# Other landing times for a planner's loads, and four moved or cut steps, in an attention, mixture-of-experts and MLP kernel

## The chip, the cores and the metric

The kernel runs on one core of a Trainium2 chip, as one launch. A core has five engines that each take their own list of instructions in order: TensorE (PE, matmuls; PEld is its weight load), VectorE (DVE), ScalarE (ACT), GpSimd (POOL) and SyncE (SP), whose list here holds only the starts of DMA transfers. They meet through semaphores. PE writes to PSUM, which has eight banks of 128 x 512 float32. The metric is the time of one execution in microseconds (us); three runs of the kernel before gave 623.84, 624.47 and 625.8, so the median is 624.47.

## The reference, cut to what matters

```python
# 1. attention: 2 batches, 8 heads, 576 positions, head size 64
rel = pos[:, None] - pos[None, :]
mask_plain = (rel >= 0) & (rel < 32)                          # heads 0 to 3
mask_dil = (rel >= 0) & (rel < 128) & (rel % 4 == 0)          # heads 4 to 7
attn = softmax(where(mask, q @ k.T / 8, -1e9)) @ v
x = attn as (1152 tokens, 512)
# 2. four experts, all of them for every token
p = domain_probs / (domain_probs.sum(-1, keepdims=True) + 1e-09)
for e in range(4):                                            # w1[e] 512x1024, w2[e] 1024x512
    out += p[:, e:e + 1] * (np.maximum(x @ w1[e], 0.0) @ w2[e])
# 3. second MLP
h = out @ w_in                                                # 512x2048
result = (h - np.tanh(h)) @ w_out                             # 2048x512, so 1152x512 float32
```

## The kernel before, in words

All products are made from operands split in a high and a low part; three matmuls (high by high, high by low, low by high) stand for one. The 1152 tokens are in two sets, set 0 of 512 and set 1 of 640. Both MLPs are walked through in slices `n` of 512 hidden columns: n = 0 to 9 belong to the four experts (0 and 1 for set 0 alone, their counterparts 8 and 9 for set 1 alone), n = 10 to 13 to the second MLP (13 is `LAST`). For a slice and a set g there are *h steps* (x by w1, 6 matmuls each, 256 columns for set 0 and 320 for set 1, gathered over several steps in PSUM sums that stay open) and *y steps* (hidden by w2, one step for each 128 tokens: 12 matmuls of 128 x 512 into one bank, which `y_sum` then adds on DVE into the tile `acc`). From slice 2 on the h steps use sums of blocks of x and w1, as in Strassen's method; six of their sums are then open at once, in six of the eight banks. `merge` puts the y steps of the slice before between the h steps: its tuple says behind how many h steps each y step stands (`FIRST`, `LATE`, `THEN`, and a literal tuple, before the loop over `steps`).

The attention of set 0 comes first. Its heads and tokens are cut in pieces: plain and dilated heads, each in two halves. `score(half, i, c)` computes scores, with i = 0 for plain and 1 for dilated; `soft`, `turn` and `use` are softmax, transposes and the product with v. Steps called with `P.fill` true, or through `fill`, may be laid in gaps: the h steps of slice 0 are the first dense work and serve as fill there. `warm` steps are matmuls on zeros that may stand in gaps (on ring `bank`). In the same stretch the weights of slices 0 and 1 arrive in `raw` tiles (512 KB each, ring of 4) and are split: the high part by a copy on ACT or DVE, the low part `w - high` by a subtraction on POOL or DVE. `emit_probs` reduces the loaded tile `pr` to `psum_r`, which gives the experts' weights `pn`.

During the experts, `d_pair(i)` decodes the second MLP's weights, 32 times: a DMA brings a tile of ring `att`, four DVE operations and one on ACT make a 128 x 512 tile `w` in one of the two slots of ring `single`, and a DMA writes `w` back to memory (`in<-att` and `out<-att` in the profile). The next decode that uses a slot must wait until its write has landed. Later `w_load` reads the decoded weights into `raw` like any others.

No order of instructions is written by hand. Every call is recorded as an operation with an estimated duration; then `Order` lays all operations: `deadlines` works out a due time for each from the PE list backwards (with `flight` as the time of a load), `lay` plays the program through a model (a load's data come at a landing time after one path of 395 KB per us, `DMA_US` behind its last byte) and takes for each engine the operation that can start first, by due time among equals, and `seek` tries shifted due times on the operations up to the end of slice 0 and keeps what the model finds no worse. `emit` then writes the instructions in the laid order. So a constant of the model moves instructions on all engines: it is no time on the chip, but it sets each engine's list. The list of PE follows the code except for fill and warm steps.

Of the kernel before, what the change touches and what calls it, by code (L numbers as in the profile page):

```python
# [219 lines left out]
class Program:  # L220


    TAIL = {"tensor": 0.24, "vector": 0.07, "scalar": 0.08, "gpsimd": 0.08, "sync": 0.0}
    DMA_US, DMA_RATE, DMA_AHEAD, DMA_DEEP = 1.35, 395.0e3, 0.45, 8

    DMA_SLOW, DMA_SLOW_RATE = 7.0, 250.0e3

# [161 lines left out]
class Order:  # L389
# [6 lines left out]
    def __init__(self, program, rounds=3):  # L396
        self.ops = program.ops
        self.program = program
        for o in self.ops:
            for b in o.before:  # L400
                self.ops[b].after.append(o.n)
        self.rings = []
        for o in self.ops:
            for t in o.tiles:
                if t.ring not in self.rings:
                    self.rings.append(t.ring)
        for ring in self.rings:
            ring.tiles.sort(key=lambda t: t.touch[0])
        self.follow = None
        self.all = program.ops  # L410
        self.from_, self.until = program.seek, program.until
        for _ in range(rounds):
            self.deadlines()
            self.lay()
        if program.seek:
            self.seek(program.seek, 1200)
        self.lay()

    def seek(self, limit, times):
# [61 lines left out]
        self.ideal = due  # L481

    def flight(self, o):
        return Program.DMA_US + o.data / Program.DMA_RATE if o.data else 0.0

    def lay(self, limit=None):

# [21 lines left out]
        while done < len(ops):  # L509
# [73 lines left out]
            if o.data:  # L583
                slow = max(path, o.end) < Program.DMA_SLOW
                path = max(path, o.end) + o.data / (Program.DMA_SLOW_RATE if slow else Program.DMA_RATE)
                come = path + Program.DMA_US
            o.landing = come
            if o.data:
                lands.append(come)
# [15 lines left out]
            for n in o.after:  # L605
                if n >= len(ops):
                    continue
                a = ops[n]
# [68 lines left out]
def tile_local_attention_moe_tanhshrink(  # L677
# [56 lines left out]
    def bank(loose=False):  # L734
        return Tile(bank_r, [128, 512], F32, loose=loose).view()
# [17 lines left out]
    def add(engine, out, a, b):  # L753
        engine.tensor_tensor(out=out, in0=a, in1=b, op=ALU.add)
# [825 lines left out]
    def y_step(kind, n, g, i):  # L1580
# [1 line left out]
        c = SETS[g][1] // 128 - 1 - i  # L1582
        first = 3 if n < EARLY else 2
        fs = {"y": range(NF), "ya": range(first), "yb": range(first, NF)}[kind]
        y = opened.pop((g, c)) if kind == "yb" else bank(P.fill)
        if kind == "ya":
            opened[g, c] = y
        for f in fs:
            hh, hl = (hts[g, f][:, i, c * 128:(c + 1) * 128] for i in range(2))
            whi, wlo = (w2t[n, f][:, i] for i in range(2))  # L1590
# [6 lines left out]
        if kind != "ya":  # L1597
            y_sum(n, g, c, y)

    def y_sum(n, g, c, y):  # L1600
        e = slices[seq[n][0]][2]
        ch = SETS[g][0] // 128 + c
        where = acc if e is not None else oacc
# [20 lines left out]
        elif new:  # L1624
            copy(t, y)
        else:
            k_ = 2 if n == LAST and g == 1 and c == 0 else 1
            for i in range(k_):
                cs = slice(i * DM // k_, (i + 1) * DM // k_)
                add(dve, t[:, cs], y[:, cs], t[:, cs])  # L1630
                if n == LAST:
                    dma(out[ch * 128:(ch + 1) * 128, cs], t[:, cs], 128 * 2048.0 / k_)

    def x2_step(g, kk):

# [39 lines left out]
            return h + [a0, a1, b0, b1] + cs[2:]  # L1675
        return h[:-1] + [a0] + h[-1:] + [a1] + cs[:1:-1] + [b0, b1]

    FIRST, LATE, THEN = (1, 2, 3, 4, 5), (3, 4, 5, 6, 8), (5, 7, 11, 13)
    steps = direct([("h", 0, 0, NF + i) for i in range(NF)], 0, 0)[:-2]
    for n in range(1, EARLY):  # L1680
        steps += direct(hs(n, 0), n, 0)
# [5 lines left out]
        steps += direct(hs(n, 1), n, 1)  # L1687
    steps += hs(N2 - 1, 1) + direct(merge(hs(N2, 0), ys(N2 - 1, 1), LATE), N2, 0) + hs(N2, 1)
    for n in range(N2 + 1, LAST + 1):
        first = (2, 3, 4, 5, 6) if n > N2 + 1 else LATE  # L1690
        steps += merge(hs(n, 0), ys(n - 1, 1), first) + merge(hs(n, 1), ys(n, 0), THEN)
    steps += ys(LAST, 1)

# [60 lines left out]
    def first_attention():  # L1754
# [13 lines left out]
        def use(half, i, c):  # L1768
            both[i].values(half, c)
# [24 lines left out]
        soft(2, 3)  # L1794
        P.fill = True
        score(1, 0)
        score(1, 1)
        P.fill = False
        turn(0)
        turn(1)  # L1800
# [5 lines left out]
        turn(3)  # L1806
        use(0, 1, 0)
        use(0, 1, 1)
        fill(*[("h", 0, 0, f) for f in range(NF)])
        soft(6)  # L1810
        turn(4)
# [159 lines left out]
```

## Time and profile before

| | value |
|---|---|
| runs | 623.84, 624.47, 625.8 us |
| profiled execution | 625.1 us, of it span 623.3 us |
| PE busy | 614.4 us, 99% of the span |
| PEld busy | 541.2 us, 87% |
| DVE, POOL, ACT busy | 62%, 51%, 49% |
| DMA over the span | 109 GB/s; 303, 366 and 311 GB/s in the first three fortieths |
| PE clock granted | full in all 40 slices |

In the timeline a line gives the start, the length, the engine, line 338 (where all engine operations are emitted; 743 for DMAs), the operation with `out<-in` tile names, shape and count, and in brackets the idle time before it with what ended it. Matmuls overlap at their ends, so the length of a PE group is longer than its share; what a step cost is the time from its start to the start of the next. A group whose count is below 12 or 6 has lost records, not matmuls.

### The profile page before, as it was taken

Reading aid. Unit: us, or ns where it says so; the run is one execution under the profiler, and the core shown is the slowest. Engines: PE = TensorE matmul, PEld = TensorE weight load, DVE = VectorE, ACT = ScalarE, POOL = GpSimd, SP = SyncE. Lnnn points to the kernel's source line nnn. Section 1 sums busy time; section 2 is a strip of 40 time slices with the busy share of each in tenths; the row PEclk is TensorE's granted clock in tenths of the full one; section 3 lists DMA queues with packets and bytes.
Section 4 is the critical chain, followed back from the end, with each engine's and each line's share of the span. In section 5 each row is a group of like instructions: output and inputs, shape, how many; then the busy total and the mean of one; then the engine's idle time right before and its main releaser. Section 6 shows DMA issues by size and latency. Waiting matters only on the chain.

```text
span 623.3 us, 10631 instructions
## 1 busy us (share of the span) xinstructions
PE 614.4 (99%) x4019; PEld 541.2 (87%) x4019; DVE 385.8 (62%) x726; ACT 305.0 (49%) x743; POOL 315.7 (51%) x281
## 2 busy tenths in 40 slices
PE   9999999999999999999999999999999999999997
PEld 5787798989888889889889889898898988998986
DVE  5855567976677877835425465446787677753652
ACT  7776774654334334414314355343774653551540
POOL 4767982854334425425425459763664662560220
PEclk9999999999999999999999999999999999999999
DMA  8993144254444555212102002330305224200012
GB/s 303 366 311 103 35 129 127 83 161 146 135 136 170 186 159 196 70 51 68 35 34 68 35 34 77 125 120 21 117 34 155 100 89 131 102 2 1 17 52 84
DMA packets 37554, 68.03 MB, mean 109 GB/s; under 512 B 4224, under 2 KB 12032, under 8 KB 37504
## 3 DMA queue, kind: packets, MB, share of 16 engines
q1 hardware_dynamic: 37216, 67.07, 32.9%
q8 instruction: 31, 0.51, 0.3%
q10 hardware_dynamic: 288, 0.30, 0.1%
q14 instruction: 19, 0.16, 0.1%
HBM read 56.61 MB, written 10.75 MB: 108 GB/s over the span
## 4 chain that ended last, share of the span: by engine, by line
PE 86%; DMA 7%; DVE 3%; issue 1%; POOL 1%; ACT 1%; SPq 1%; DVEq 0%; POOLq 0%; ACTq 0%
PE bank L338 86%; DMA raw<-in_moe_w_dram 3%; DMA out<-att 2%; DVE att L338 2%; DMA pr<-in_moe_domain_probs_dram 1%; DMA x<-in_k_dram 1%; DVE acc L338 1%; DMA in<-att 1%; SPq L743 1%; ACT w L338 0%; POOL w L338 0%; DVE w L338 0%; POOL att L338 0%; POOL x L338 0%; DVE bank L338 0%
## 5 line engine op out<-in xcount | busy, mean ns | idle before, releaser
L338 PE MATMUL bank<-w,h 128*128 128x512 f32 (+1 forms) x1392 | 324.6, 385 | 2.9 <-DVE acc L338 1.0
L338 PE MATMUL bank<-x,w 128*128 128x256 f32 (+2 forms) x1992 | 287.3, 298 | 0.9 <-DVE bank L338 0.9
L338 PEld LDWEIGHTS bank<-w,h 128*128 128x128 f32 (+1 forms) x1392 | 240.4, 184 | 54.9 <-DVE acc L338 2.1
L338 PEld LDWEIGHTS bank<-x,w 128*128 128x128 f32 x1992 | 277.7, 188 | 11.3 <-DVE bank L338 1.1
L338 POOL TENSOR_TENSOR w<-raw,w 128x512 fp32r<-128x512 f32 x102 | 135.9, 1344 | 146.0 <-ACT w L338 141.9
L338 ACT ACTIVATE h<-bank 128x320 fp32r<-128x320 f32 (+3 forms) x168 | 68.4, 421 | 78.8 <-PE bank L338 62.5
L338 DVE SCALAR_TENSOR_TENSOR acc<-bank,pn,acc 128x512 f32<-128x512 f32 x59 | 44.2, 749 | 67.8 <-PE bank L338 67.8
L338 DVE SCALAR_TENSOR_TENSOR att<-att 128x512 int32<-128x512 int32 (+1 forms) x96 | 84.1, 887 | 2.1 <-ACT att L338 0.5
L338 DVE TENSOR_TENSOR bank<-bank,p 128x320 f32<-128x320 f32 (+1 forms) x132 | 61.1, 466 | 33.3 <-PE bank L338 20.0
L338 ACT ACTIVATE w<-raw 128x512 fp32r<-128x512 f32 x108 | 66.9, 628 | 24.4 <-PE bank L338 22.6
L338 DVE SCALAR_TENSOR_TENSOR h<-bank,h 128x320 fp32r<-128x320 f32 (+2 forms) x124 | 55.6, 463 | 26.1 <-ACT h L338 24.8
L338 POOL TENSOR_TENSOR w<-sum,w 128x512 fp32r<-128x512 f32 x36 | 48.5, 1346 | 43.2 <-ACT w L338 42.1
L338 ACT ACTIVATE p<-bank 128x320 f32<-128x320 f32 (+1 forms) x88 | 35.6, 412 | 50.6 <-PE bank L338 49.7
L338 ACT ACTIVATE att<-bank 128x256 f32<-128x256 f32 (+3 forms) x78 | 32.6, 431 | 52.1 <-PE bank L338 42.3
L338 ACT ACTIVATE att<-att 128x512 f32<-128x512 f32 (+2 forms) x39 | 25.4, 655 | 37.5 <-DVE att L338 31.7
L338 DVE TENSOR_TENSOR acc<-bank,acc 128x512 f32<-128x512 f32 (+1 forms) x28 | 18.7, 670 | 30.9 <-PE bank L338 30.9
L338 POOL TENSOR_TENSOR sum<-raw 128x512 f32<-128x512 f32 x12 | 15.5, 1292 | 39.1 <-DMA raw<-in_moe_w_dram 19.0
L338 POOL TENSOR_TENSOR h<-att,h 128x256 fp32r<-128x256 f32 (+1 forms) x28 | 21.8, 801 | 25.4 <-ACT h L338 24.8
L338 ACT ACTIVATE w<-sum 128x512 fp32r<-128x512 f32 x36 | 22.6, 627 | 21.0 <-PE bank L338 16.5
L338 DVE TENSOR_SCALAR att<-att 128x512 int32<-128x512 int32 x32 | 16.4, 511 | 21.7 <-DMA out<-att 11.4
L338 POOL TENSOR_TENSOR att<-att,st 128x480 f32<-128x480 f32 (+1 forms) x20 | 18.9, 948 | 9.9 <-DVE st L338 9.4
L338 DVE TENSOR_TENSOR bank<-bank,att 128x256 f32<-128x256 f32 (+1 forms) x32 | 14.7, 463 | 10.1 <-ACT att L338 9.9
(73 smaller groups left out, 348.4 us busy)
## 6 DMA issues: line engine op xcount, KB each, us to landing
raw<-in_moe_w_dram SPq DMA_DIRECT2D x40, 512.0 KB, 3.9
att<-in_moe_w_in_dram SPq DMA_DIRECT2D x16, 512.0 KB, 4.4
att<-in_moe_w_out_dram SPq DMA_DIRECT2D x16, 512.0 KB, 4.5
in<-att SPq DMA_DIRECT2D x16, 256.0 KB, 4.1
out<-att SPq DMA_DIRECT2D x16, 256.0 KB, 4.1
raw<-in SPq DMA_DIRECT2D x8, 512.0 KB, 3.6
raw<-out SPq DMA_DIRECT2D x8, 512.0 KB, 3.7
h<-in_v_dram SPq DMA_DIRECT2D x7, 512.0 KB, 7.1
```

The lines of the kernel that those rows point to most:

```text
L338: getattr(self.engine, method)(**real)
L743: getattr(nc, queue).dma_start(out=a, in_=b)
```

## The change: landing times by stretch, a moved score, other merge places, a cut last chunk

`DMA_US` is no longer 1.35 us for every load but goes by the model's time: 1.35 until 12 us, 2.2 until 28, 3.2 until 42 and 2.8 after; `flight` has 2.5; `seek` makes 1000 tries instead of 1200. The second dilated score, `score(1, 1)`, is called behind the first values as fill. `LATE` and the literal tuple of `merge` change. The last y step of the program is made in two banks of 256 columns, each with its own add and write; `y_sum` gets the columns as an argument.

```diff
-    DMA_US, DMA_RATE, DMA_AHEAD, DMA_DEEP = 1.35, 395.0e3, 0.45, 8
+    DMA_RATE, DMA_AHEAD, DMA_DEEP = 395.0e3, 0.45, 8
+    DMA_US = (12.0, 1.35), (28.0, 2.2), (42.0, 3.2), (9e9, 2.8)
...
-            self.seek(program.seek, 1200)
+            self.seek(program.seek, 1000)
...
     def flight(self, o):
-        return Program.DMA_US + o.data / Program.DMA_RATE if o.data else 0.0
+        return 2.5 + o.data / Program.DMA_RATE if o.data else 0.0
...
-                come = path + Program.DMA_US
+                come = path + next(us for until, us in Program.DMA_US if path < until)
...
+        if (n, g, c) == (LAST, 1, 0):
+            for i in range(2):
+                y = bank()
+                for f in fs:
+                    hh, hl = (hts[g, f][:, j, c * 128:(c + 1) * 128] for j in range(2))
+                    whi, wlo = (w2t[n, f][:, j, i * 256:(i + 1) * 256] for j in range(2))
+                    with P.group():
+                        for m, (a, b_) in enumerate(((hh, whi), (hh, wlo), (hl, whi))):
+                            pe.matmul(
+                                out=y[:, :256], lhsT=a, rhs=b_,
+                                start=(f == 0 and m == 0), stop=(f == NF - 1 and m == 2),
+                            )
+                y_sum(n, g, c, y[:, :256], slice(i * 256, (i + 1) * 256))
+            return
...
-            k_ = 2 if n == LAST and g == 1 and c == 0 else 1
-            for i in range(k_):
-                cs = slice(i * DM // k_, (i + 1) * DM // k_)
-                add(dve, t[:, cs], y[:, cs], t[:, cs])
-                if n == LAST:
-                    dma(out[ch * 128:(ch + 1) * 128, cs], t[:, cs], 128 * 2048.0 / k_)
+            add(dve, t[:, cs], y, t[:, cs])
+            if n == LAST:
+                dma(
+                    out[ch * 128:(ch + 1) * 128, cs], t[:, cs], 512.0 * (cs.stop - cs.start),
+                )
...
-    FIRST, LATE, THEN = (1, 2, 3, 4, 5), (3, 4, 5, 6, 8), (5, 7, 11, 13)
+    FIRST, LATE, THEN = (1, 2, 3, 4, 5), (3, 4, 5, 7, 9), (5, 7, 11, 13)
...
-        first = (2, 3, 4, 5, 6) if n > N2 + 1 else LATE
+        first = FIRST if n > N2 + 1 else LATE
...
         score(1, 0)
-        score(1, 1)
         P.fill = False
...
         use(0, 1, 1)
+        P.fill = True
+        score(1, 1)
+        P.fill = False
         fill(*[("h", 0, 0, f) for f in range(NF)])
```

What the constants move shows in the engines' lists. On SP, the two v tiles of the first halves and both w1 tiles of slice 0 now stand ahead of the q tile (256 KB) and the two k tiles (192 KB each) of the second dilated half, with the first w2 tile between those k tiles; before, the q and k tiles came first. On PE, three warm matmuls are added (10 for 7). The PE list has 12 matmuls of 512 columns fewer and 24 of 256 more.

The DVE list near the 25th us, before; `w2` and `raw` are the weights of slice 0, `x0` a block of set 0's x that PE waits for:

```order
L338 TENSOR_REDUCE psum_r_530<-pr_421 128x9
L338 TENSOR_TENSOR w2_455<-raw_253,w2_455 128x512
L338 TENSOR_TENSOR w2_532<-raw_262,w2_532 128x512
L338 TENSOR_TENSOR psum_r_530<-psum_r_530,eps_81 128x9
L338 TENSOR_TENSOR x0_364<-bank_534,x0_359 128x256
```

and now:

```order
L340 TENSOR_TENSOR w2_437<-raw_236,w2_437 128x512
L340 TENSOR_REDUCE psum_r_543<-pr_424 128x9
L340 TENSOR_TENSOR w2_530<-raw_303,w2_530 128x512
L340 TENSOR_TENSOR x0_338<-bank_534,x0_327 128x256
L340 SCALAR_TENSOR_TENSOR h0_583<-bank_453,h0_583 128x256
L340 TENSOR_TENSOR psum_r_543<-psum_r_543,eps_75 128x9
```

One of the two subtractions that stood behind the reduction of `pr` stands ahead of it, and the addition of `eps` behind the block of x.

The DVE list near the 175th us, before; `att` are steps of two decodes, `acc1` the sums of set 1's y steps, whose banks they give back:

```order
L338 SCALAR_TENSOR_TENSOR acc1_1776<-bank_2255,pn_594,acc1_1776 128x512
L338 TENSOR_SCALAR att_1483<-att_2193 128x512
L338 TENSOR_SCALAR att_1483<-att_2272 128x512
L338 SCALAR_TENSOR_TENSOR acc1_1776<-bank_2291,pn_594,acc1_1776 128x512
L338 SCALAR_TENSOR_TENSOR att_1483<-att_2272,att_1483 128x512
L338 SCALAR_TENSOR_TENSOR att_1483<-att_2193,att_1483 128x512
```

and now:

```order
L340 SCALAR_TENSOR_TENSOR acc1_1770<-bank_2260,pn_614,acc1_1770 128x512
L340 SCALAR_TENSOR_TENSOR acc1_1770<-bank_2292,pn_614,acc1_1770 128x512
L340 TENSOR_SCALAR att_1489<-att_2188 128x512
L340 TENSOR_SCALAR att_1489<-att_2275 128x512
L340 SCALAR_TENSOR_TENSOR att_1489<-att_2275,att_1489 128x512
L340 SCALAR_TENSOR_TENSOR att_1489<-att_2188,att_1489 128x512
```

The first two operations of the next pair of decodes have gone behind one more sum.

The PE list in the last slice, before; 128x256 rows are h steps of set 0 into their sums, 128x512 rows y steps of set 1:

```order
L338 MATMUL bank_6184<-x0_4136,w1_5972 128x256 x6
L338 MATMUL bank_6192<-w2_5774,h1_5978 128x512 x3
L338 MATMUL bank_6192<-w2_5780,h1_6014 128x512 x3
L338 MATMUL bank_6192<-w2_5791,h1_6034 128x512 x3
L338 MATMUL bank_6192<-w2_5799,h1_6048 128x512 x3
L338 MATMUL bank_6207<-x0_4136,w1_5972 128x256 x6
L338 MATMUL bank_6216<-w2_5774,h1_5978 128x512 x3
L338 MATMUL bank_6216<-w2_5780,h1_6014 128x512 x3
L338 MATMUL bank_6216<-w2_5791,h1_6034 128x512 x3
L338 MATMUL bank_6216<-w2_5799,h1_6048 128x512 x3
L338 MATMUL bank_6100<-x0_4123,w1_6003 128x256 x6
```

and now:

```order
L340 MATMUL bank_6201<-x0_4139,w1_5979 128x256 x6
L340 MATMUL bank_6209<-w2_5764,h1_5984 128x512 x3
L340 MATMUL bank_6209<-w2_5770,h1_6017 128x512 x3
L340 MATMUL bank_6209<-w2_5776,h1_6037 128x512 x3
L340 MATMUL bank_6209<-w2_5786,h1_6051 128x512 x3
L340 MATMUL bank_6231<-x0_4139,w1_5979 128x256 x6
L340 MATMUL bank_6103<-x0_4126,w1_6006 128x256 x6
L340 MATMUL bank_6132<-x0_4126,w1_6006 128x256 x6
```

The last y step (6216, now 6209) has gone from behind the h step that opens the sixth sum (6207, now 6231) to ahead of it.

## Rows read from the trace of the kernel before

**Rows 1.** The page: an engine's busy time, share and instructions.

```profile
PE 614.4 (99%) x4019; PEld 541.2 (87%) x4019; DVE 385.8 (62%) x726; ACT 305.0 (49%) x743; POOL 315.7 (51%) x281
```

**Rows 2.** Timeline of PE, 0 to 60 us: start, length, operation, idle before.

```profile
11.65 0.89 PE L338 MATMUL bank<-x,x 64*64 64x96 f32 x32
...
17.04 0.39 PE L338 MATMUL bank<-w,h 96*64 96x64 f32 x6 [0.72 <-issue]
...
17.76 5.24 PE L338 MATMUL bank<-x,w 128*128 128x256 f32 x42
...
28.90 1.68 PE L338 MATMUL bank<-w,h 128*128 128x512 f32 x6 [0.83 <-DVE x L338]
...
54.20 0.64 PE L338 MATMUL bank<-ident,att 128*96 128x128 f32 x4 [0.35 <-POOL att L338]
```

**Rows 3.** Timeline of DVE, around the reduction of `pr`.

```profile
25.46 0.19 DVE L338 TENSOR_REDUCE psum_r<-pr 128x9 f32<-128x36 f32 x1 [0.27 <-DMA pr<-in_moe_domain_probs_dram]
...
25.57 2.86 DVE L338 TENSOR_TENSOR w<-raw,w 128x512 fp32r<-128x512 f32 x2
...
28.43 0.41 DVE L338 TENSOR_TENSOR x<-bank,x 128x256 fp32r<-128x256 f32 x1
```

**Rows 4.** Timeline of DVE, the second w1 tile's first use.

```profile
17.20 0.43 DVE L338 CAST w<-raw 128x512 fp32r<-128x512 f32 x1 [0.52 <-DMA raw<-in_moe_w_dram]
```

**Rows 5.** Windows: busy time by engine, clock, DMA share, GB/s.

```profile
10.00:20.00 10.00, 8.93 (x141) 7.33 (x137) 7.25 (x23) 8.55 (x30) 6.51 (x7) 1.00 1.03 392
```

**Rows 6.** DMA view, 0 to 30 us: KB each, median from issue to landing.

```profile
h<-in_v_dram SPq DMA_DIRECT2D x4, 512.0 KB, 9.0
```

**Rows 7.** Timeline of POOL, 30 to 60 us.

```profile
50.66 1.29 POOL L338 TENSOR_TENSOR sum<-raw 128x512 f32<-128x512 f32 x1 [4.26 <-DMA raw<-in_moe_w_dram]
```

**Rows 8.** Timeline of PE, 156 to 190 us.

```profile
176.45 0.88 PE L338 MATMUL bank<-x,w 128*128 128x256 f32 x6
177.16 2.95 PE L338 MATMUL bank<-w,h 128*128 128x512 f32 x12
179.96 0.87 PE L338 MATMUL bank<-x,w 128*128 128x256 f32 x6
181.15 3.05 PE L338 MATMUL bank<-w,h 128*128 128x512 f32 x12 [0.32 <-DVE acc L338]
184.22 3.09 PE L338 MATMUL bank<-x,w 128*128 128x256 f32 x24
188.23 2.04 PE L338 MATMUL bank<-x,w 128*128 128x256 f32 x15 [0.92 <-DVE bank L338]
```

**Rows 9.** Timeline of DVE, 156 to 190 us.

```profile
178.65 0.43 DVE L338 TENSOR_SCALAR att<-att 128x512 int32<-128x512 int32 x1 [3.59 <-issue]
180.01 0.43 DVE L338 TENSOR_SCALAR att<-att 128x512 int32<-128x512 int32 x1 [0.93 <-DMA in<-att]
180.35 0.74 DVE L338 SCALAR_TENSOR_TENSOR acc<-bank,pn,acc 128x512 f32<-128x512 f32 x1
```

**Rows 10.** Timeline of PE at four places of the second MLP's merges.

```profile
423.74 0.86 PE L338 MATMUL bank<-x,w 128*128 128x256 f32 x6
424.74 2.60 PE L338 MATMUL bank<-w,h 128*128 128x512 f32 x10
...
473.98 0.86 PE L338 MATMUL bank<-x,w 128*128 128x256 f32 x6
474.83 2.36 PE L338 MATMUL bank<-w,h 128*128 128x512 f32 x9
...
524.35 0.86 PE L338 MATMUL bank<-x,w 128*128 128x256 f32 x6
525.92 3.05 PE L338 MATMUL bank<-w,h 128*128 128x512 f32 x12 [0.71 <-DVE acc L338]
...
572.68 0.86 PE L338 MATMUL bank<-x,w 128*128 128x256 f32 x6
573.63 3.05 PE L338 MATMUL bank<-w,h 128*128 128x512 f32 x12
```

**Rows 11.** Timeline of DVE, the last two adds of the program.

```profile
619.85 0.76 DVE L338 TENSOR_TENSOR acc<-bank,acc 128x256 f32<-128x256 f32 x2 [2.09 <-PE bank L338]
```

More of the change, by code (lines that the diff above doesn't have):

```diff
@@ L1584, in y_step @@
         fs = {"y": range(NF), "ya": range(first), "yb": range(first, NF)}[kind]
-        y = opened.pop((g, c)) if kind == "yb" else bank(P.fill)
+        if (n, g, c) != (LAST, 1, 0):
+            y = opened.pop((g, c)) if kind == "yb" else bank(P.fill)
         if kind == "ya":
             opened[g, c] = y
+        if (n, g, c) == (LAST, 1, 0):
[12 more added lines that the diff above has]
+            return
         for f in fs:
@@ L1598, in y_step, with y_sum @@
             y_sum(n, g, c, y)
-    def y_sum(n, g, c, y):
+    def y_sum(n, g, c, y, cs=slice(0, DM)):
         e = slices[seq[n][0]][2]
```

## The prediction

> **What bounds the kernel now.** I read the page first: PE is busy for 614.4 of 623.3 us [rows 1], so what can be won lies in the rest, or in PE steps that run longer than their like. Busy time hides the second kind, because matmuls overlap: between 423.74 and 424.74 no idle time is given before the next group, yet the h step there took 1.00 us from start to start [rows 10], where the same step from 176.45 to 177.16 took 0.71 [rows 8]. So next I went through the PE timeline by starts and compared every step with its like: 0.71 us for an h step of 6 matmuls of 256 columns, and 2.80 for a y step of 12 of 512 (177.16 to 179.96) [rows 8]. Excess stands in three places: the head up to 60 us (waits of 0.72, 0.83 and 0.35) [rows 2], 180 to 188 us [rows 8], and four h steps of the second MLP [rows 10]. Last I read the engine that PE waits for at each of them, DVE or POOL [rows 3, 7, 9]. The clock is full throughout, 1.00 in the stretch shown [rows 5], so no term here is one of clock.
>
> The profiled execution took 625.1 us (span 623.3, and 1.8 around it), 0.6 over the median of 624.47. I take all differences from the trace and put them on the median.
>
> **The change part by part.**
>
> *Head.* At 28.90 PE has waited 0.83 us for a block of x [rows 2]. DVE made it at 28.43, behind the reduction of `pr` (25.46, after a wait for its load) and two subtractions of weights that took 2.86 together, 1.43 each [rows 3]. In the new DVE list one of the two stands ahead of the reduction, where DVE had been waiting, and the addition of `eps` stands behind the block. If `pr` lands as before, what follows it is 0.19 + 1.43 + 0.41, so the block is there at 27.5; with a subtraction of up to 1.77, when POOL works beside it, at 27.85. PE must come earlier too: it came at 28.07 (28.90 less 0.83). The dilated scores that moved, 0.89 us at 11.65, stand ahead of the first dense step no more, and the wait of 0.72 at 17.04, which I put on a v tile still under way, goes because that tile is loaded sooner; 17.76 becomes about 16.15 [rows 2]. The 0.89 comes back between the dense steps, so PE is some 0.75 ahead at 28 and waits at 27.3. It starts at 27.55 to 27.85 instead of 28.90: 1.05 to 1.35 won, taken as 1.2.
>
> Are the weights there at 16.15? The second w1 tile was first used at 17.20, as it landed [rows 4]. Now 640 KB less stand ahead of it, at 392 GB/s [rows 5] 1.67 us, so it lands near 15.5. The moved k tiles now have the same bytes ahead as that tile had before, without one k tile (192 KB, 0.5 us) for the first, and with a w2 tile (512 KB, 1.3 us) for the second: 16.7 and 18.5. PE wants them behind one h step (16.9) and behind three more and the first scores (19.1). Both are covered, by a few tenths only. Bounds: all that PE can win here is 28.90 less 27.3, 1.6; if a k tile is late by 1.3 us more than this the head ends 0.5 later than before.
>
> *POOL at 54.* PE waited 0.35 [rows 2] for a multiply on POOL queued behind a sum that had itself waited 4.26 for a load [rows 7]. In the new POOL list that multiply stands ahead of the sum: 0.35 won. Bound below: nothing, if the softmax ahead of it is late instead.
>
> *Decoding.* DVE stands still from 174.6 to 178.65 and again to 180.01, for a slot of `single` whose write is under way [rows 9]; the sum queued behind comes only at 180.35, and PE, whose y step needs that sum's bank, starts at 181.15 instead of 180.67. The h step at 179.96 thus took 1.19 (0.48 over its like), the y step 3.07 (0.27 over), and the four h steps from 184.22 took 4.01 against 2.84 (1.17 over), ending in a wait for DVE [rows 8]: 1.92. With one more sum ahead of the waiting operations, that sum no longer waits for a write, and the first two excesses, 0.75, go. The third is a backlog: the sum after that one was begun at 183.42 before; now it follows three steps of the decode from 180.44 on, at 0.62 each, so at 182.3, 1.1 earlier, which is nearly the 1.17. I take 0.95 of it, so 1.7. Queued behind the waiting operations now: one sum fewer and the same bank additions. Bounds 0.75 to 1.92.
>
> *Merges.* Six sums of the h steps hold six banks, so two are left for y steps. The y step behind the sixth opened sum needs the bank of the y step ahead, whose add on DVE (0.74 for a like one [rows 9]) is not done in one h step of 0.71. That is the excess of 0.29, 0.14, 0.86 and 0.24 at the four places [rows 10], 1.53, and the y step behind runs 3.05 instead of 2.95 at the two where all its records are there, +0.1 each. In the new order the last y step stands ahead of the sixth sum in three slices, and in the fourth two h steps lie between. All goes: 1.53 + 0.2 = 1.7, bounds 1.4 and 1.95 (0.1 at all four).
>
> *The last chunk.* The two adds that end the program take 0.76 together [rows 11]; of 256 columns each, one now runs beside the second bank's matmuls, and the rest is 0.42. That wins 0.34. The 12 matmuls of 512 took 2.80, and 24 of 256, at 0.71 for 6, take 2.84 [rows 8]: 0.04 lost. With up to 0.05 for the change of bank I take 0.25 won, bounds 0.1 and 0.34. The Trainium skill, "TensorE: Matmul & The Clock Gate", section "Back-to-back issue gap", speaks against this edit: it says that a sustained stream costs about 81 ns a matmul at 128 columns and about 131 ns at 512. Between the two, an estimate from that page is 98 ns for 256, so 24 of these would cost 0.77 us more than 12 of 512, and the edit would lose 0.4. The rows measure 118 and 233 ns, nearly in the ratio of the columns, since the three float32 passes are no such stream; the sum by the page would be 0.65 us higher than mine.
>
> *What may be late next.* The new lists have tight places too: weight splits between sums of set 1 late in the second MLP, a chain of three decodes near 125 us with little slack, and three more warm matmuls, which only pay where PE waits anyway. None shows in a row of before. I take 0.4 lost, with 0 and 1.5 as ends; the upper is near the largest stall that such a chain caused here, 1.17 [rows 8].
>
> Sum: -1.2 - 0.35 - 1.7 - 1.7 - 0.25 + 0.4 = -4.8, from 624.47 to **619.7 us** (in the profiled execution's own terms 620.3).
>
> **The rivals.**
>
> *A: the head wins more.* PE comes earlier at every place of the head, and the remaining waits go as well: 1.6 instead of 1.2, and 0.3 of further waits, with the other terms at their good ends (1.92, 1.95, 0.34, and no new stall). -1.6 - 0.3 - 0.35 - 1.92 - 1.95 - 0.34 = -6.5, so 618.0. For it: each term is read from a wait that is in the trace. Against it: the softmax between is a chain over ACT, DVE and POOL, DVE and ACT are the busiest engines of the second ten microseconds after PE [rows 5], and starting PE sooner does not shorten it.
>
> *B: the landing constants do nothing on the chip.* They change what the planner believes, not when data land. If `pr` and the v tiles land so that the head's gain is taken back at the next wait, and the writes of decoded weights stall DVE at another sum, only merges and last chunk remain: -1.7 - 0.25 + 0.4 = -1.55, so 622.9. For it: DVE's waits at 178.65 and 180.01 are for transfers [rows 9], which an order of DVE does not shorten. Against it: both moved places have PE work beside the wait now.
>
> *C: slower, by the moved k tiles.* PE takes its list in order, so a k tile that lands late stops the dense steps behind it as well. If the tile lands not by the bytes ahead of it but with the rest of what is queued then, as late as `pr` did (25.46 [rows 3]), PE waits from 19.1 to 25.5, 6.4 us, and the head's 1.2 is lost: -4.8 + 1.2 + 6.4 = +2.8, so 627.3. It turns the sign from a landing at 22.7 on. For it: v tiles of that stretch took 9.0 us from issue to landing [rows 6], and another such delay behind these would do. Against it: issued near 9.5, 9.0 more is 18.5, the same as by bytes. The Trainium skill, "DMA: Bandwidth & Descriptors", section "Queues, rings and completion order", says that completion is not first in, first out for an issuing engine, so a landing by bytes ahead is not assured; no row here separates the two.
>
> **How the numbers follow.** A change of under 0.3%, 1.9 us, can't be told from none. The forecast has a chance of 0.60, its own range 618.0 to 621.5; A has 0.12, B 0.20, C 0.08. Of B a third counts as faster (better than 622.6), the rest as same. So faster is 0.60 + 0.12 + 0.07 = 0.79, same 0.13, slower 0.08. The range goes from 617.2, below A by a little since its terms may add to more, to 623.3, which holds most of B and leaves out C.
>
> **What would show it.** Right: no wait of PE for x near 28, with `pr`'s reduction between the two subtractions; dense steps from about 16.2; no gap at 54; y steps of 2.80 and h steps of 0.71 right through 180 to 188 us; in the second MLP's merges all h steps of set 0 at 0.71; one add of 256 columns behind the last matmul. Wrong: PE waiting at the moved scores for a load (C), the head ending no sooner than before although it starts dense sooner (B), a new wait for DVE where decodes stand, or 24 matmuls at the end that take more than 2.95.

## The result, and the profile after

Six runs of the changed kernel took 618.73 to 619.66 us, median 619.18; six of the kernel before, beside them, had a median of 624.79. The ratio is 0.9907, with a 95% interval of 0.9891 to 0.9922: 0.8 to 1.1% faster, beyond the 0.3% set as the bound of noise. Against the 624.47 that the forecast started from, it is 5.3 us; against the runs beside it, 5.6. The forecast was 619.7, the profiled execution 619.3 (forecast in those terms: 620.3).

The page of the changed kernel: engine shares, then the shares of the chain of work that ended last. The last line is that chain in the kernel before.

```profile
PE 612.9 (99%) x4034; PEld 542.4 (88%) x4034; DVE 375.2 (61%) x726; ACT 307.8 (50%) x743; POOL 317.7 (51%) x281
...
PE 98%; DVE 1%; ACT 0%; POOL 0%; issue 0%; DVEq 0%; POOLq 0%; ACTq 0%
```

```profile
PE 86%; DMA 7%; DVE 3%; issue 1%; POOL 1%; ACT 1%; SPq 1%; DVEq 0%; POOLq 0%; ACTq 0%
```

PE's busy time fell by only 1.5 us [rows 1]; the rest of the 5.8 us of span was time between steps. The chains tell more: that of the kernel before held 7% of DMA and 86% of PE, this one holds no DMA.

The PE timeline after, at the places of [rows 2]:

```profile
16.42 1.00 PE L340 MATMUL bank<-x,w 128*128 128x256 f32 x6
17.36 0.56 PE L340 MATMUL bank<-x,x 64*64 64x96 f32 x16
17.85 1.68 PE L340 MATMUL bank<-x,w 128*128 128x256 f32 x12
19.46 0.56 PE L340 MATMUL bank<-x,x 64*64 64x96 f32 x16
19.95 3.11 PE L340 MATMUL bank<-x,w 128*128 128x256 f32 x24
...
28.24 1.65 PE L340 MATMUL bank<-w,h 128*128 128x512 f32 x6
...
53.00 0.60 PE L340 MATMUL bank<-ident,att 128*96 128x128 f32 x4
```

No row has a wait left. The dense steps start at 16.42 (before: 17.76), the step of 28.90 at 28.24, that of 54.20 at 53.00. Its DVE and POOL queues, against [rows 3, 7]:

```profile
25.74 0.19 DVE L340 TENSOR_REDUCE psum_r<-pr 128x9 f32<-128x36 f32 x1 [0.88 <-DMA pr<-in_moe_domain_probs_dram]
...
26.80 0.41 DVE L340 TENSOR_TENSOR x<-bank,x 128x256 fp32r<-128x256 f32 x1
```

```profile
46.42 1.29 POOL L340 TENSOR_TENSOR sum<-raw 128x512 f32<-128x512 f32 x1 [0.63 <-DMA h<-in_v_dram]
...
50.15 1.00 POOL L340 TENSOR_TENSOR att<-att,st 128x480 f32<-128x480 f32 x1
```

The block of x is ready at 27.2, a microsecond before PE comes. `pr` even landed later than before (25.74 for 25.46), and it no longer matters. On POOL the sum starts at 46.42 instead of 50.66, so PE's multiply is not held up behind it. (Its row names a v tile as what ended the wait; the sum's own tile was issued at 39.64, where before it was issued at 43.87, and took 6.7 us to land in both.)

The stretch of the decodes, PE and DVE, against [rows 8, 9]:

```profile
175.77 2.94 PE L340 MATMUL bank<-w,h 128*128 128x512 f32 x12
178.54 0.88 PE L340 MATMUL bank<-x,w 128*128 128x256 f32 x6
179.26 2.96 PE L340 MATMUL bank<-w,h 128*128 128x512 f32 x12
182.06 8.15 PE L340 MATMUL bank<-x,w 128*128 128x256 f32 x65
...
192.83 2.95 PE L340 MATMUL bank<-w,h 128*128 128x512 f32 x12
```

The last of these y steps, in the kernel before:

```profile
196.29 2.96 PE L338 MATMUL bank<-w,h 128*128 128x512 f32 x12
```

DVE in the changed kernel:

```profile
175.26 0.75 DVE L340 SCALAR_TENSOR_TENSOR acc<-bank,pn,acc 128x512 f32<-128x512 f32 x1 [2.73 <-PE bank L340]
176.78 0.43 DVE L340 TENSOR_SCALAR att<-att 128x512 int32<-128x512 int32 x1 [0.77 <-DMA in<-att]
177.46 0.43 DVE L340 TENSOR_SCALAR att<-att 128x512 int32<-128x512 int32 x1 [0.25 <-DMA in<-att]
```

DVE's waits for the writes are 0.77 and 0.25 where they were 3.59 and 0.93, and PE runs through. PE was 1.39 us ahead of before at the y step of 177.16 (now 175.77) and 3.46 ahead at that of 196.29 (now 192.83): this stretch took 17.06 us instead of 19.13, so it gave 2.07 against this one trace of before.

In the second MLP, against [rows 10, 11]: one of the merges, the one new wait, and the end.

```profile
520.38 2.94 PE L340 MATMUL bank<-w,h 128*128 128x512 f32 x12
523.15 7.15 PE L340 MATMUL bank<-x,w 128*128 128x256 f32 x58
...
457.26 3.30 PE L340 MATMUL bank<-x,w 128*128 128x320 f32 x24 [0.37 <-DVE bank L340]
...
613.14 0.42 DVE L340 TENSOR_TENSOR acc<-bank,acc 128x256 f32<-128x256 f32 x1 [0.72 <-PE bank L340]
614.55 0.42 DVE L340 TENSOR_TENSOR acc<-bank,acc 128x256 f32<-128x256 f32 x1 [0.99 <-PE bank L340]
```

### The profile page after: what moved, and what is told of

Same layout as the page of the kernel before. It is cut to its first block, busy times and chain, and to the rows that moved or that the text cites. A ratio compares the mean times of both kernels' runs of the same rounds, so it can differ in the third digit from the quotient of the medians.

```text
span 617.5 us, 10655 instructions
## 1 busy us (share of the span) xinstructions
PE 612.9 (99%) x4034; PEld 542.4 (88%) x4034; DVE 375.2 (61%) x726; ACT 307.8 (50%) x743; POOL 317.7 (51%) x281
## 4 chain that ended last, share of the span: by engine, by line
PE 98%; DVE 1%; ACT 0%; POOL 0%; issue 0%; DVEq 0%; POOLq 0%; ACTq 0%
PE bank L340 98%; DVE x L340 0%; ACT att L340 0%; DVE bank L340 0%; DVE st L340 0%; POOL att L340 0%; DVE acc L340 0%; DVE att L340 0%; DVE h L340 0%; DVE zero L340 0%; DVEq L340 0%; POOLq L340 0%; ACTq L340 0%
## 5 line engine op out<-in xcount | busy, mean ns | idle before, releaser
L340 PE MATMUL bank<-w,h 128*128 128x512 f32 (+2 forms) x1404 | 323.5, 383 | 0.0
L340 ACT ACTIVATE h<-bank 128x320 fp32r<-128x320 f32 (+4 forms) x168 | 69.0, 422 | 79.7 <-PE bank L340 65.7
L340 DVE SCALAR_TENSOR_TENSOR att<-att 128x512 int32<-128x512 int32 (+1 forms) x96 | 73.1, 777 | 1.3
L340 ACT ACTIVATE att<-att 128x512 f32<-128x512 f32 (+2 forms) x39 | 25.3, 658 | 22.7 <-DVE att L340 16.9
L340 ACT ACTIVATE acc<-bank 128x512 f32<-128x512 f32 (+4 forms) x27 | 12.9, 505 | 11.7 <-PE bank L340 11.2
```

The source lines that it names most:

```text
L340: getattr(self.engine, method)(**real)
```

## The experiments

Each ran beside the kernel before on its chip. The ratios of whole times have intervals of 0.2 to 0.7 percentage points in width, so terms under 1 us are read from traces. A trace shows a single wait to a few hundredths, but only of its own execution. The ratio is the one on record; it is not the quotient of the two medians and differs from it by up to 0.1 percentage points. Where two orders of a list are compared, the operations were moved after the planner had laid everything else, so nothing else moves; a move gives an operation, by its number, a start behind another's.

**s_head: DVE's order near 25 us alone.** (78 is the reduction of `pr`, 79 to 81 the rest of the probabilities.)

```diff
+        for n, behind in ((78, 360), (79, 328), (80, 79), (81, 80)):
+            self.ops[n].start = self.ops[behind].start + 0.0001
         for o in sorted(self.ops, key=lambda o: (o.start, o.n)):
```

> The kernel before, with only the DVE list changed near 25 us: the reduction of pr goes behind the first of the two weight subtractions, the rest of the probabilities behind the two operations on x and h that followed. Loads, scores and PE stay. My theory (DVE's queue made PE late at 28.90): the block of x is ready by 27.5 to 27.9, PE comes at 28.07 and no longer waits 0.83, and the time falls by 0.7 to 0.85 us. Rival (the head gain of the changed kernel came from the loads and the moved score alone, because DVE is late for another reason): PE still waits, as DVE's subtraction itself waits for its weights; less than 0.2 us won.

Measured: 624.0 against 624.26, ratio 0.9996 (0.9979 to 1.0014). DVE, PE and POOL in its trace:

```profile
26.82 0.41 DVE L338 TENSOR_TENSOR x<-bank,x 128x256 fp32r<-128x256 f32 x1
```

```profile
27.71 1.62 PE L338 MATMUL bank<-w,h 128*128 128x512 f32 x6
...
54.00 0.64 PE L338 MATMUL bank<-ident,att 128*96 128x128 f32 x4 [1.39 <-POOL att L338]
```

```profile
50.46 1.30 POOL L338 TENSOR_TENSOR sum<-raw 128x512 f32<-128x512 f32 x1 [3.46 <-DMA raw<-in_moe_w_dram]
...
52.96 0.99 POOL L338 TENSOR_TENSOR att<-att,st 128x480 f32<-128x480 f32 x1
```

At 28.9 the theory held: the wait of 0.83 is gone. The step comes 1.19 sooner, but 0.35 of that is not the edit's: the dense steps, which it doesn't touch, began at 17.41 in this execution and at 17.76 before. At 54 nearly all was given back: POOL's sum waits for a load, and starts at 50.46 (50.66 before [rows 7]) although PE is a microsecond ahead, so the wait of 0.35 [rows 2] became 1.39. That wait is not the same in each execution: with the head unchanged it was 0.92 in the trace of s_dec, and that of e_tail gives none.

**s_head_pool: the same, and POOL's multiply ahead of the sum.**

```diff
+        self.ops[409].start = self.ops[602].start - 0.0001
```

> The DVE order of s_head, and on POOL the multiply that PE waited for at 54 laid ahead of the sum that waits for its load. Where s_head started the step of 28.90 at 27.71 and then waited 1.39 at 54.00, my theory (two queues, one behind the other: what DVE gives, POOL's wait for the load takes back) says that the lead of 1.2 now stays: no wait near 53, 1.1 to 1.6 us won at 57 us and at the end. Rival (the load itself, or the softmax ahead of the multiply, is what is late): PE still waits near 53 and no more than 0.4 is won.

Measured: 623.23 against 624.16, ratio 0.9994 (0.9976 to 1.0011). PE in its trace:

```profile
53.01 0.60 PE L338 MATMUL bank<-ident,att 128*96 128x128 f32 x4
```

No wait near 53, and PE is 1.19 us ahead of [rows 2] there, the same as in the changed kernel (53.00): 0.66 at the step of 28.90 (both traces have it at 28.24) and 0.53 behind it. The mechanism is shown. The whole time does not show it clearly: that trace has another wait of 0.48 at 112 us and the one near 188, and its ten runs spread over 5 us. Near 188 it loses less than before, though its list there is the old one. The second decode operation:

```profile
178.25 0.43 DVE L338 TENSOR_SCALAR att<-att 128x512 int32<-128x512 int32 x1 [0.37 <-DMA in<-att]
```

It comes 1.61 behind its y step (at 176.64 here), where it came 2.85 behind before, and the stretch of 19.13 took 17.91.

**s_dec: the decode's two operations behind one more sum.**

```diff
+        for n, behind in ((1129, 1032), (1169, 1129)):
+            self.ops[n].start = self.ops[behind].start + 0.0001
```

> The kernel before, with only the DVE list changed near 175 us: the first two operations of the pair of decodes stand behind the next sum of a y step. My theory: the stall on the write-back no longer holds that sum, the excess of 0.48 and 0.27 at 179.96 and 181.15 goes, and most of the 1.17 behind 184.22: 1.7 to 2.1 us won. Rival (the wait for the writes only moves to the next sum): the 1.17 stays, 0.75 won, or nothing where the next y step waits in its place.

Measured: 623.87 against 624.26, ratio 0.9985 (0.9965 to 1.0005). DVE and PE in its trace:

```profile
177.30 0.75 DVE L338 SCALAR_TENSOR_TENSOR acc<-bank,pn,acc 128x512 f32<-128x512 f32 x1 [1.83 <-PE bank L338]
180.21 0.43 DVE L338 TENSOR_SCALAR att<-att 128x512 int32<-128x512 int32 x1 [2.15 <-DMA in<-att]
180.90 0.43 DVE L338 TENSOR_SCALAR att<-att 128x512 int32<-128x512 int32 x1 [0.27 <-DMA in<-att]
```

```profile
181.32 2.95 PE L338 MATMUL bank<-w,h 128*128 128x512 f32 x12
184.57 3.09 PE L338 MATMUL bank<-x,w 128*128 128x256 f32 x24 [0.30 <-DVE acc L338]
188.60 1.57 PE L338 MATMUL bank<-x,w 128*128 128x256 f32 x11 [0.94 <-DVE bank L338]
```

The y step at 181.32 is on time, but the next sum waits instead, and the loss at 188 is the old one (0.94 for 0.92 [rows 8]). The rival was right: my swap moves the wait and wins little. The stretch took 18.85 here, 17.06 in the changed kernel. Its list is not yet the changed one: four steps of the decode stand here between the two waiting operations and the next sum, three in the changed kernel.

**e3_constants: only the planner's landing times, flight and tries.** Its edit is the first four pieces of the diff of the change.

> The kernel before, with only the planner's landing times, flight and tries changed; the code of the steps is the same. Theory 1 (the landing times lay work behind a wait for a DMA later, and so take DMAs off PE's path): the waits near 29, 54 and 188 go, the chain's share of DMA falls from 7% to under 2%, 2.5 to 4 us won; the four waits of the merges stay. Theory 2 (the new orders are one draw of the random search, and the moved score does the head): the head is no better than before, the stretch near 188 still loses 1.1, under 1 us won.

Measured: 620.87 against 624.16, ratio 0.9946 (0.9931 to 0.9962), 3.3 us. Its chain, and DVE near the decodes:

```profile
PE 98%; DVE 1%; ACT 0%; issue 0%; DVEq 0%
```

```profile
175.78 0.75 DVE L340 SCALAR_TENSOR_TENSOR acc<-bank,pn,acc 128x512 f32<-128x512 f32 x1 [2.73 <-PE bank L340]
176.44 0.75 DVE L340 TENSOR_SCALAR att<-att 128x512 int32<-128x512 int32 x2
```

Theory 1: no wait for a write is left there, and the chain holds no DMA. The SP lists say why. The writes of the decode before, in the kernel before and in this one:

```profile
174.24 2.08 SPq L743 DMA_DIRECT2D in<-att  x2
```

```profile
171.28 0.98 SPq L745 DMA_DIRECT2D in<-att  x2
```

With PE 0.88 us ahead here at the y step of 177.16, the writes go out 2.1 us sooner by PE's steps (in the changed kernel too: 170.77, with PE 1.39 ahead). The order of DVE is also the changed one here, with the sum ahead of the two decode operations, so this run does not separate the order from the sooner writes; nor does it separate the landing times from the other number of tries. The four waits of the merges (0.30, 0.14, 0.24, 0.24) stayed. In the head it is 0.4 ahead by 54 us, a third of the changed kernel's 1.2.

**e4b_score: only the moved score.** Its edit is the last two pieces of that diff.

> The kernel before, with only the second dilated score moved behind the first values as fill; landing times as before. Theory 1 (landing times decide): the wait near 188 stays as it was, about 1.1; in the head the dense steps start earlier by 0.9 to 1.5, but a wait for a load or for a queue behind one takes it back by 60 us; within 0.7 us of before. Theory 2 (the moved score makes the head's gain): 0.7 to 1.3 won by 60 us and kept.

Measured: 622.67 against 624.16, ratio 0.997 (0.9953 to 0.9986), 1.5 us. In its trace PE is 0.71 ahead at 54, without a wait there, and the excess near 188 is 1.06, against 1.17 before. The two smaller ones ahead of it, 0.48 and 0.27 before, are not in this trace, so the stretch took 18.25 instead of 19.13. Theory 2 for the head, theory 1 for the wait at 188; its list came from a new search too, so the 0.7 is not the score's alone.

**e1_merges and e2_old_merges: the merge tuples alone, added to the kernel before, and taken back in the changed one.**

```diff
-    FIRST, LATE, THEN = (1, 2, 3, 4, 5), (3, 4, 5, 6, 8), (5, 7, 11, 13)
+    FIRST, LATE, THEN = (1, 2, 3, 4, 5), (3, 4, 5, 7, 9), (5, 7, 11, 13)
-        first = (2, 3, 4, 5, 6) if n > N2 + 1 else LATE
+        first = FIRST if n > N2 + 1 else LATE
```

> The kernel before, with only the places of the second products in the second MLP's merges changed (the two tuples). The planner lays all behind 417 us anew. My theory (one bank too few for the last y step): the four excesses of 0.29, 0.14, 0.86 and 0.24 go, and 0.1 behind each, so 1.5 to 1.95 us won; if the new stall of 0.6 us near 457 that the changed kernel has comes with this edit, and the old one of 0.28 near 465 goes, 1.2 to 1.6. Rival (it is DVE that is late, and the wait moves to the next y step): under 0.5 won.

Measured: 624.06 against 624.26, ratio 0.9996 (0.9979 to 1.0012). The four waits are gone from its trace, and a new one of 0.54 stands at 462.73, where the changed kernel has it at 457. That trace also has a wait of 0.88 at 237 and one of 0.72 at 487 that no other here has. The first lies ahead of 417, where PE, DVE and ACT have the lists of the kernel before, so it is this execution's; whose the second is stays open. The whole time tells nothing. From the y step of 384.66 to the end the trace took 237.64, with that second wait, against 238.04 to 238.13 in the four others with the old merges, the old last chunk and the landing times of before (s_head, s_dec, s_head_pool, e4b_score), and 238.67 in that of the kernel before.

> The changed kernel with the old places of the second products in the second MLP's merges; all up to 417 us stays. Theory 1 (banks): the four waits of 0.3, 0.14, 0.24 and 0.24 come back, with 0.1 behind each, while the stall of 0.53 at 457 may go for the old one of 0.28 at 465: 0.8 to 1.4 us slower than the changed kernel, so about 620.0 to 620.6. Theory 2 (the merges' gain is given back by the new stall): within 0.3 of the changed kernel.

Measured: 620.26, that is 1.08 over the changed kernel's 619.18; ratio to before 0.9921 (0.9891 to 0.9951). The first of the four in its trace:

```profile
420.06 0.88 PE L340 MATMUL bank<-x,w 128*128 128x256 f32 x6
421.07 3.07 PE L340 MATMUL bank<-w,h 128*128 128x512 f32 x12
```

The four waits are back, at 0.29, 0.13, 0.23 and 0.23 over the like step; the 0.53 at 457 is gone and the old 0.21 at 461 is there. Together the waits are 0.88; 0.88 + 4 x 0.1 (the slower y steps behind them) + 0.21 - 0.53 = 0.96, which is what the trace loses from 417 us on, near the 1.08 of the medians. Theory 1.

**e_tail and e_tail4: the last chunk in two banks, and in four.** e_tail puts the changed `y_step` and `y_sum` alone into the kernel before; e_tail4 goes on from the changed kernel.

> The kernel before, with only the last chunk by two banks of 256 columns, each with its own add and write. My theory: the last matmul ends within 0.1 us of where it did, and one add of 0.42 follows instead of two in 0.76, so 0.25 to 0.4 us won. Rival (24 matmuls of 256 columns cost markedly more than 12 of 512, as the Trainium skill, page TensorE: Matmul & The Clock Gate, section Back-to-back issue gap, would have it by its figures): the last matmul ends 0.7 later, and 0.3 to 0.4 us is lost.

Measured: 623.87 against 624.26, ratio 0.9984 (0.9972 to 0.9996). In its trace the first add of 256 columns starts at 616.86 and the second at 618.28: 1.42 for 12 matmuls of 256, 118 ns each, so twice that is 2.84 for what took 2.80. Lined up at the last step that both share, the last add ends 0.29 sooner. My theory.

```diff
-            for i in range(2):
+            for i in range(4):
...
-                    whi, wlo = (w2t[n, f][:, j, i * 256:(i + 1) * 256] for j in range(2))
+                    whi, wlo = (w2t[n, f][:, j, i * 128:(i + 1) * 128] for j in range(2))
...
-                y_sum(n, g, c, y[:, :256], slice(i * 256, (i + 1) * 256))
+                y_sum(n, g, c, y[:, :128], slice(i * 128, (i + 1) * 128))
```

> The changed kernel with the last chunk in four banks of 128 columns instead of two of 256. Theory 1 (a matmul's time goes nearly by its columns, 118 ns for 256 and 233 for 512): 48 of 128 take 2.9 to 3.1 us where 24 took 2.8, and the last add is 0.25 instead of 0.42: within 0.2 of the changed kernel. Theory 2 (the weight load for each matmul sets a floor; the Trainium skill, page TensorE: Matmul & The Clock Gate, section Back-to-back issue gap, gives about 81 ns at 128 columns): 48 take 3.9, and 0.8 to 0.9 us are lost.

Measured: 621.84, 2.66 over the changed kernel. Its last adds:

```profile
613.68 0.29 DVE L340 TENSOR_TENSOR acc<-bank,acc 128x128 f32<-128x128 f32 x1 [0.60 <-PE bank L340]
...
617.70 0.29 DVE L340 TENSOR_TENSOR acc<-bank,acc 128x128 f32<-128x128 f32 x1 [1.05 <-PE bank L340]
```

The four follow each other by 1.34, the time of 12 matmuls of 128 columns: 112 ns each, against 118 for twice the columns. Four times 1.34 less 2.84 is 2.5; the shorter last add gives back 0.13, which leaves 2.4. The trace has 2.3 from the start of the last y steps on, the medians 2.66. So 128 columns cost nearly what 256 do, as a floor under them would have it, but theory 2 had the loss at a third of its size. That the weight load sets the floor is not shown. The 112 ns are more than is stated by the Trainium skill: "TensorE: Matmul & The Clock Gate", section "Back-to-back issue gap", gives 81 ns at 128 columns.

**x_late_k: what rival C would cost.** The changed kernel with the two moved k tiles (19, 18) issued behind a w2 tile and two v tiles more.

```diff
+        for n, behind in ((19, 23), (18, 19)):
+            self.ops[n].start = self.ops[behind].start + 0.0001
```

> The changed kernel with the two k tiles of the second dilated half issued behind one w2 tile and two v tiles more (1.5 MB) on SP. If a tile lands by the bytes ahead of it, the first comes some 4.5 us later than 16.7 and the second 4 us later than 18.5: 21 to 22.5, so PE, which takes its list in order, stands at the first moved score from 17.4 to 21 or 22, and 3.5 to 4.5 us are lost. If tiles land out of order by more than a microsecond, PE waits less than 3. If the mechanism of my rival C is wrong (something else covers), the time stays within 1 us.

Measured: 625.25, 6.1 over the changed kernel. PE, and the stretches around the wait (busy time by engine, granted clock):

```profile
21.61 0.92 PE L340 MATMUL bank<-x,x 64*64 64x96 f32 x16 [4.16 <-DMA x<-in_k_dram]
22.46 2.93 PE L340 MATMUL bank<-x,w 128*128 128x256 f32 x12
25.32 0.92 PE L340 MATMUL bank<-x,x 64*64 64x96 f32 x16
26.17 3.19 PE L340 MATMUL bank<-x,w 128*128 128x256 f32 x24
```

```profile
12.00:17.00 5.00, 5.00 (x77) 3.60 (x74) 3.86 (x13) 4.12 (x14) 3.38 (x4) 1.00 1.05 402
17.00:21.60 4.60, 0.45 (x4) 0.24 (x3) 2.93 (x5) 2.14 (x6) 3.47 (x4) 0.77 1.04 407
...
22.40:25.30 2.90, 2.90 (x16) 2.63 (x12) 0.00 (x0) 0.00 (x0) 0.00 (x0) 0.50 1.11 302
...
26.20:29.20 3.00, 3.00 (x29) 3.00 (x26) 2.88 (x8) 1.91 (x8) 1.07 (x2) 0.98 0.61 220
```

The tile came when its place by bytes said (21 to 22), and the wait was 4.16, as expected. The loss was larger than the wait, 6.3 us by 30 us in the trace, because the clock fell: the first moved score came 4.25 late, and of the 2.1 more that were lost 2.0 lie in the steps up to 26.17 that ran at the lower clock (last section).

**x_nowarm: the changed kernel without its four warm matmuls behind 10 us.**

```diff
+        for o in self.ops:
+            o.gone = o.gone or o.fill == "idle" and o.start > 9.0
```

> The changed kernel without its four warm matmuls behind 10 us (each a product of zeros; the result is not changed by them). Theory 1 (they lie in gaps in which PE waits for the softmax anyway): PE's dense steps start within 0.2 of 16.4, and the time is the same within 0.3, at the full granted clock. Theory 2 (they stand in PE's way): the dense steps start 0.5 to 1.2 sooner. Theory 3 (they hold the clock up): the granted clock falls somewhere between 10 and 17 us and the start is later.

Measured: 619.32, the same as the changed kernel. The dense steps start 0.29 sooner, at 16.13, and PE waits 0.26 for x at 28.20, so both reach that step within 0.04. The granted clock is 1.00 in each of five stretches from 0 to 30. The start lies between what theories 1 and 2 had; the time is theory 1's: the warm matmuls cost nothing, and here they gave nothing. One row of its DVE matters for the decodes:

```profile
178.07 0.43 DVE L340 TENSOR_SCALAR att<-att 128x512 int32<-128x512 int32 x1 [1.56 <-DMA in<-att]
```

The second decode operation waits longer here than in the changed kernel, 2.35 behind its y step (175.72) for 1.69, and PE still runs through: 17.07 for the stretch (192.79 less 175.72).

**x_best: the new wait at 457 taken out.**

```diff
+        for n, behind in ((2123, 2101),):
+            self.ops[n].start = self.ops[behind].start + 0.0001
```

> The changed kernel, with one DVE operation of x2's blocks near 454 us laid some 3.5 us earlier, where DVE is idle for 1.86, so that the bank that PE waits for at 457.26 is given back 0.4 earlier. Theory (DVE's queue makes that wait): it falls from 0.53 to 0.1 or 0.2, against the kernel before 6.0 us won instead of 5.6. Rival (the two subtractions beside POOL's, 1.98 for both, fill what is freed): the wait stays over 0.4.

Measured: 619.15, ratio to before 0.992 (0.9905 to 0.9935). In the trace the excess fell from 0.53 to 0.13, and the span from 617.5 to 617.0. By the trace it is 0.4 better than the changed kernel; by the median, 619.15 against 619.18, nothing can be told.

## Why the prediction was right, and where not

The sum was right, -4.8 forecast and -5.6 measured (-5.3 from the forecast's own base), and so were the likeliest case and the sign. Its terms were less right than their sum: head and merges gave less than forecast, the decodes more, and that these errors nearly cancel is luck.

| step | forecast | measured, and in what |
|---|---|---|
| head, and POOL at 54, together | -1.55 | -1.2 at 54 us, of it -0.66 at 28.90 (changed kernel; s_head_pool the same) |
| decoding | -1.7 | -2.07 against the trace of before, -0.85 to -1.83 against five others of the old order; the swap alone (s_dec) still loses 1.79 of it |
| merges, with the new stall | -1.7 + 0.4 | -1.08 (e2_old_merges) |
| last chunk | -0.25 | -0.29 (e_tail) |

*Head.* The queue on DVE was what made PE late: with the order alone the step came at 27.71 (s_head). In the changed kernel it came at 28.24 and not at the forecast 27.55 to 27.85, since PE was later, not x. The dense steps started at 16.42, not 16.15; the moved scores took 0.98, not 0.89; and 42 matmuls of h steps took 5.49 between 16.42 and 22.89 (6.47 less the 0.98), where they took 5.12 in the trace of before. That they are now cut by other work explains little of it: uncut, with the old list, they took 5.36 to 5.46 in the traces of s_head, s_head_pool, s_dec, e1_merges and e_tail. I had carried the block over at the price of one execution.

*The two head terms are one.* I summed the wait at 28.90 and the wait at 54.20 as separate gains. s_head shows that the first is worth little without the second, 0.20 in its trace: behind it stands a queue on POOL with a load that did not come sooner because PE did. My sum came out because both were removed; had POOL's order stayed, the step "1.2 won" would have failed nearly in full. What is late next was asked for the softmax and not for this queue, though the row of its wait was on the table [rows 7].

*Decoding.* This is the step that failed: "With one more sum ahead of the waiting operations, that sum no longer waits for a write, and the first two excesses, 0.75, go", and the backlog of 1.17 with them. s_dec made just that swap, and the next sum waited in its place. (A slip of reading beside it: DVE stood still from 175.06, not from 174.6, as 178.65 less 3.59 gives [rows 9].) The runs show three things in its place.

First, the writes: in the changed kernel the decode before finishes sooner, and its writes go out 2.1 us sooner by PE's steps; e3_constants does this without the other edits.

Second, the order: sooner writes are not all of it. With the old list the stretch from the y step of 177.16 to that of 196.29 took longer the later the second decode operation came behind its y step: 17.91 at 1.61 us (s_head_pool), 18.25 and 18.27 at 1.97 (e4b_score, e_tail), 18.83 at 2.53 (e1_merges), 18.89 at 2.60 (s_head), 19.13 at 2.85 (before). With the changed list it took 17.06 at 1.69, and 17.07 at 2.35 (x_nowarm, where the first of the two came early). So the changed order bears a wait that the old one does not, but the swap alone does not make that order. Whether the third decode step in place of the fourth ahead of the next sum does it, no run shows.

Third, the size: 1.92 came from the trace in which the old order lost most of six, so the 2.07 measured against it is the upper end of what this stretch gave.

Rival B, that landing constants move nothing on the chip, is wrong: with flight and tries, and without the other edits, they are worth 3.3 us of the 5.6.

*Merges.* The mechanism (one bank too few) is shown by the traces of e1 and e2: the four waits go and come with the tuples. The size is off, because most of the 0.86 at 525.92 [rows 10] belonged to that one execution: in every trace with the old merges since (s_head, s_dec, e_tail, s_head_pool, e3_constants, e4b_score, e2_old_merges) it is 0.23 to 0.25, like its three fellows. 0.30 + 0.14 + 0.24 + 0.24 + 0.4 is 1.3. The 0.4 allowed for tight places was 0.53 less the 0.21 to 0.28 of the old one near 465.

*Last chunk.* As worked out. The estimate from the Trainium skill's figures would have turned this edit into a loss; at 256 columns the rows decided. At 128 (e_tail4) there is a loss, larger than those figures give. Why the rows differ from them, which the prediction put down to the float32 passes, no run shows.

*Rival C* did not come: PE does not wait at the moved scores. Its price, microsecond for microsecond of the wait, was too low: in x_late_k 4.16 of wait cost 6.1, since the clock fell as well.

Not explained: 0.24 us that PE gains evenly between the y steps of 196.29 and 384.66, where both lists run without waits. It is not one execution's: the six traces of the old order that have no wait there took 188.34 to 188.47, the six of the changed one 188.12 to 188.18.

## What to carry to other kernels

Before adding up waits, line the program up at its later steps: a wait that is removed is a gain only if PE is still ahead behind the next queue that ends in a transfer. Where an order is laid by a model, its landing times are worth measuring: here later ones (with other tries and flight) were worth 3.3 us and took the transfers out of the chain. And take the size of a single wait from more than one execution: here one of four like waits was 0.86 in the trace that the forecast used and 0.23 to 0.25 in seven others, and one stall of 1.92 was 0.7 to 1.7 in five others.

## What the runs showed of the hardware

A wait of PE can cost more than its length. In x_late_k PE stood still for 4.16 us, and from 22.4 to 25.3 the granted clock was 0.50, the lower of the two levels (1.2 GHz), after 1.00 in the busy stretch ahead of the wait. 12 matmuls of 256 columns went from 17.85 to 19.46 in the changed kernel, 1.61 us; here they took 2.86, and twice 16 scores took 0.85 each instead of 0.49. PE worked on without a gap, and from 26.2 to 29.2 the clock was 0.98. The wait of 0.72 at 17.04 in the kernel before left it at 1.00 [rows 2, 5].

In these streams at full clock a matmul of 128 columns cost 112 ns (e_tail4), one of 256 cost 118 (e_tail) and one of 512 cost 233 (2.80 for 12), so going from 256 to 128 columns saved almost nothing.

The kernels whose chain holds more DMA scattered more. The runs of s_head, s_dec, e1_merges and s_head_pool, ten of each, spread over 2.9 to 5.0 us (6 to 9% of DMA in the chain of the profile), those of e_tail and e4b_score, ten each, over 1.8 and 1.5 (6 and 5%), and eight of x_late_k over 2.2 (3%). The changed kernel, e3_constants, e2_old_merges, e_tail4, x_nowarm and x_best, with 0%, spread over 0.3 to 1.1 us, in four to eight runs each. The traces show one such place: the stretch of the decodes took 17.91 to 19.13 us with the old list, and 17.06 to 17.08 in all six traces of the changed one.
